# A fused windowed-attention and gated-MLP kernel: its hand-written order of steps is written anew

## Chip, cores and metric

The kernel runs on one core of a Trainium2 chip. The metric is the device time of one execution in microseconds (us). Five engines with queues of their own work side by side, each in the order in which its instructions were issued: PE (matrix products and transposes through the array), DVE, ACT and POOL (vector work; POOL also issues the loads that change the data type), and SP (which only issues transfers).

## The reference

The first half is attention over four batches of 8 heads, 768 positions and 64 channels. A position sees the 128 positions up to itself and the first four ("sinks"). The second half is a gated MLP with a product over the positions, on the attention's output.

```python
scores = scale * np.matmul(q, k.transpose(0, 1, 3, 2))
keep = is_sink | in_window                      # 4 sinks, a window of 128
a = softmax(np.where(keep, scores, -1e9))
x = (a @ v)  as [B, S, H * D]                   # [4, 768, 512]
h = gelu_tanh(x @ w_in)                         # [4, 768, 1024]
u, v = h[..., :512], h[..., 512:]
v_n = (v - mean) / sqrt(var + 1e-6) * g_ln
v_s = einsum('ts,bsd->btd', w_sg, v_n) + b_sg   # w_sg is 768 x 768
out = x + (u * v_s) @ w_out
```

Inputs and output are float32; the kernel works in bf16 and sums in float32.

## The kernel before, in words

**One list is the program.** The string `STEPS` names some 670 steps, and a loop at the end of the kernel issues them one by one. A name is the function, then its indices, then perhaps a letter for the engine (`A` ACT, `D` DVE, `P` POOL). The list is the only thing that sets the order on each engine's queue; waits between engines follow from which tiles the steps read and write. The batches are interleaved by hand: the MLP of one batch runs beside the attention of the next.

**Attention of batch b**, with head pair p (0 to 3):
- `LPQ`/`LPK` (batch 0, SP, float32, one head pair each, cast by `CPQ`/`CPK`), `LQ`/`LK` (other batches, POOL, cast on the way, one position tile each): loads of q and k. `LVH.b.i` loads v for four heads (POOL). `LC` (SP) and `VSM` (DVE) make the sinks' rows of v; `ZERO` sets the columns of ones in the two `v_sb` tiles and clears `ks_sink`; `VSO`, `VSK`, `FILL`, `MASK`, `MASK0`, `IDEN`, `IDEN2` set constants.
- `TQ`/`TK` transpose on PE into a `mm` tile, `EQ`/`EK` copy out to `qT`/`kT`. For batch 0 their second index is the head pair; for 1 and 2 it is a pair of position tiles; for batch 3 `DQ`/`DK` (SP) do it as transposing transfers.
- `QK.b.p.g` writes scores of position-tile group g (0 to 2) into a `sc` tile, `EX` takes the exponential (ACT) into a `P` tile, `MK` masks it (DVE, or two selects on POOL). A fifth index 1 in `QK` adds the mask as a product instead. `KS`, `SK`, `SX` do the same for the sinks.
- `AV.b.p.k` multiplies P with v, whose column of ones gives the sums; `NR` divides and writes `x_sb` (DVE). k runs over three groups of two position tiles in batch 0, over two groups of three in the others.

**MLP of batch b:** `XT`/`XE` (batch 0, PE and a copy) or `XD.b.half` (SP, a transposing transfer) turn x. `MV.b.g` and `MU.b.g` are the products with the two halves of w_in for two position tiles, `GV`/`GU` their gelu (ACT); `BN`, `RS` (a power, POOL), `NM` and `Z` normalise v. `WT`/`WE` transpose w_sg. `SP.b.hf.dc` is the product over positions, `GT` scales it and adds b_sg (DVE), `GM` multiplies by u (DVE or POOL). `OU.b.t` multiplies with w_out, `RA` adds x into an `ot` tile (DVE), `ST` stores it. `SH` stores halves of its columns; for the last tile (batch 3, tile 5) `OH` and `RH` also work by halves. `LW.0` loads the half of w_in that `MV` reads, `LW.1` the other, `LWS` w_sg, `LWO` w_out, `LG` g_ln, `LB` b_sg, `GTR`/`GCP` turn g_ln.

**Tiles.** PSUM has two `sc` tiles (two banks each) and four `mm` tiles (one bank each); a step that needs one takes the next in turn (`fresh`), and must wait until whoever read it last is done. `P` has 10 tiles, `ot` 6, `gtmp` 4, `vt` 3; q, k, v, their transposes, x and z have two each, one per batch in turn.

**Constant products.** `HM.n` makes the next `fresh` issue n products with the zero tile `warm` into the fresh tile first. They compute nothing that is kept.

**Table loads.** ACT holds one table of functions at a time; exponential and gelu are in different ones. `TBL.G` and `TBL.E` run a one-column activation ahead of need.

```python
    def fresh(ring, key):
        t = ring.new(key)
        for _ in range(pre[0]):
            nc.tensor.matmul(t if ring is mm_ring else t[:, 0, :], warm[:, 0:128], warm, start=True, stop=True)
        pre[0] = 0
        return t
```

Of the kernel before, what the change touches and what calls it, by code (L numbers as in the profile page):

```python
# [45 lines left out]
RA.0.3 DK.3.0 SP.1.0.0 RA.0.4 SX.2.0 EX.2.0.1 SP.1.0.1 GT.1.0.0 DQ.3.0 EX.2.1.1 GM.1.0.0.D SP.1.1.0 MK.2.0.1.P
GT.1.0.1 QK.2.2.1 ST.0.3 GT.1.1.0 QK.2.3.1 GM.1.0.1.P DQ.3.1 EX.2.2.1 AV.2.0.0 SP.1.1.1 MK.2.1.1.D EX.2.3.1 MK.2.2.1.P
NR.2.0.0 AV.2.1.0 QK.2.0.2 DQ.3.2 QK.2.1.2 KS.3 EX.2.0.2 MK.2.3.1.P NR.2.1.0 SP.1.1.2 GT.1.1.1 EX.2.1.2 OU.0.5
MK.2.0.2.P GT.1.1.2 ST.0.0 ST.0.4 QK.2.2.2 RA.0.5 QK.2.3.2 MK.2.1.2.P EX.2.2.2 AV.2.2.0 AV.2.3.0 NR.2.2.0 SP.1.1.3
# [666 lines left out]
```

## Time and profile before

| | |
|---|---|
| median of 3 runs | 155.8 us (155.4 to 155.85) |
| the profiled execution | 155.89 us, of which its span is 154.2 us |
| busy in the span | PE 145.7 us (95%), DVE 122.9 (80%), ACT 100.0 (65%), POOL 99.7 (65%) |
| PE products | 1540, weight loads 1554 |
| granted clock | 1.0 |
| loads by POOL (q0) | 11.01 MB in 64608 packets |
| transfers by SP (q1) | 13.41 MB in 22552 packets |

The span runs from the first to the last instruction. A line such as `L483` is a line of the kernel: the scores are L483 (L478 adds a mask), their exponential L488, masks L495 on DVE and L498/L501 on POOL, AV is L524/L528/L531, NR L540/L541, MV L566, MU L607, SP L627, GT L632, GM L637, OU L644, RA L648, OH L657, RH L661; loads by POOL are L225 (q, k), L271 (v), L277 (w_in), L282 (w_sg), L285 (w_out); the constant products are L190, TBL is L309, and copies and casts L199 (ACT), L200 (DVE) and L204 (POOL). In the lines of the page's second part each digit is the busy share of a fortieth of the span, in tenths.

### The profile page before, as it was taken

The numbers are of one execution on the slowest core, as the hardware profiler recorded it, in microseconds if no ns is written. First come the engines' busy times: TensorE is split into PE (matmuls) and PEld (weight loads), VectorE is DVE, ScalarE is ACT, GpSimd is POOL, SyncE is SP. The second block draws the span as 40 slices with busy tenths as digits, with TensorE's granted clock in tenths as the row PEclk, the third lists the DMA queues.
The fourth block names the chain that finished last, engine by engine and source line by source line (L and its number), as shares of the span: only waits on it lengthen the run. The fifth ranks groups of instructions, "written<-read, shape, count | busy, mean of one in ns | idle before, by whom it ended". The sixth has DMA issues, their size and how long they took to land.

```text
span 154.2 us, 3867 instructions
## 1 busy us (share of the span) xinstructions
PE 145.7 (95%) x1540; PEld 94.5 (61%) x1554; DVE 122.9 (80%) x296; ACT 100.0 (65%) x117; POOL 99.7 (65%) x127
## 2 busy tenths in 40 slices
PE   6899899999999988999899999999999999999990
...
GB/s 158 305 351 157 154 195 204 166 189 211 148 141 154 185 155 140 147 150 156 156 223 250 81 276 177 185 190 81 211 72 1 105 221 73 150 54 20 0 203 206
DMA packets 87178, 24.67 MB, mean 160 GB/s; under 512 B 78772, under 2 KB 84920, under 8 KB 87160
## 3 DMA queue, kind: packets, MB, share of 16 engines
q0 software_dynamic: 64608, 11.01, 95.7%
q1 hardware_dynamic: 22552, 13.41, 33.0%
q8 instruction: 12, 0.20, 0.5%
q14 instruction: 6, 0.05, 0.1%
...
## 4 chain that ended last, share of the span: by engine, by line
PE 54%; POOL 18%; DMA 15%; ACT 4%; DVE 4%; issue 2%; SPq 1%; DVEq 0%; ACTq 0%; POOLq 0%
PE mm L627 15%; DMA v_sb<-in_v_dram 11%; PE mm L644 10%; PE sc L566 9%; PE sc L607 8%; POOL q L225 5%; POOL k L225 4%; DMA uT<-in_k_dram 4%; PE sc L483 4%; PE mm L524 3%; POOL v_sb L271 3%; PE mm L528 2%; POOL wsg_gated L637 2%; POOL P L498 2%; POOL P L501 2%
## 5 line engine op out<-in xcount | busy, mean ns | idle before, releaser
L488 ACT ACTIVATE P<-sc 128x1024 bf16<-128x1024 f32 (+1 forms) x48 | 43.4, 952 | 10.3 <-PE sc L483 10.1
L627 PE MATMUL mm<-wsgT,z 128*128 128x384 bf16 x192 | 34.4, 327 | 0.3 <-ACT z L597 0.3
L627 PEld LDWEIGHTS <-z 128*128 128x128 bf16 x192 | 17.6, 98 | 12.5 <-issue 0.7
L570 ACT ACTIVATE vt<-sc 128x1024 f32<-128x1024 f32 x12 | 12.3, 1027 | 18.4 <-PE sc L566 18.4
L632 DVE SCALAR_TENSOR_TENSOR gtmp<-mm,g_sb,b_bc 128x384 bf16<-128x384 f32 x32 | 19.0, 610 | 4.2 <-PE mm L627 4.0
L637 POOL TENSOR_TENSOR wsg_gated<-gtmp,uT 128x384 bf16<-128x384 bf16 x15 | 14.9, 1006 | 11.3 <-DVE gtmp L632 11.2
L607 PE MATMUL sc<-xT,w_in_sb 128*128 128x256 bf16 x192 | 22.1, 273 | 0.0
L566 PE MATMUL sc<-w_in_sb,xT 128*128 128x512 bf16 x92 | 21.8, 379 | 0.2
L644 PE MATMUL mm<-w_out_sb,wsg_gated 128*128 128x512 bf16 x85 | 21.2, 379 | 0.5
L498 POOL TENSOR_SCALAR_AFFINE_SELECT P<-P 128x512 bf16<-128x512 bf16 x21 | 13.7, 653 | 11.4 <-ACT P L488 11.4
L607 PEld LDWEIGHTS <-w_in_sb 128*128 128x128 bf16 x192 | 18.7, 98 | 2.9
L579 DVE BATCH_NORM_STATS2 st<-vt 128x6 f32<-128x512 f32 x24 | 15.4, 685 | 6.1 <-ACT vt L570 6.0
L541 DVE TENSOR_TENSOR x_sb<-mm,rcp 128x384 bf16<-128x384 f32 (+1 forms) x36 | 18.5, 513 | 1.2
L588 POOL TENSOR_TENSOR rs<-rs,neg_half 128x4 f32<-128x4 f32 (+1 forms) x8 | 7.1, 882 | 15.8 <-DVE rs L583 14.4
L225 POOL DMA_DIRECT2D k<-in_k_dram x18 | 16.4, 924 | 1.3 <-DMA v_sb<-in_v_dram 1.3
L648 DVE TENSOR_TENSOR ot<-mm,x_sb 128x512 f32<-128x512 f32 x23 | 15.4, 683 | 2.2 <-PE mm L644 2.2
L225 POOL DMA_DIRECT2D q<-in_q_dram x18 | 16.8, 956 | 0.0
L524 PE MATMUL mm<-v_sb,P 128*128 128x65 bf16 x192 | 16.1, 194 | 0.6 <-DVE x_sb L541 0.4
L524 PEld LDWEIGHTS <-P 128*128 128x128 bf16 x192 | 14.5, 97 | 2.5 <-DMA v_sb<-in_v_dram 0.6
L528 PE MATMUL mm<-v_sb,P 128*128 128x65 bf16 x160 | 15.4, 193 | 0.4 <-POOL P L501 0.4
L612 ACT ACTIVATE uT<-sc 128x1024 bf16<-128x1024 f32 x12 | 12.2, 1024 | 5.1 <-PE sc L607 5.1
L566 PEld LDWEIGHTS <-xT 128*128 128x128 bf16 x96 | 9.2, 98 | 10.1
...
## 6 DMA issues: line engine op xcount, KB each, us to landing
...
```

The costliest lines, as they stand in the source:

```text
L225: return nc.gpsimd.dma_start(out=dst.rearrange("p (h d) -> p h d", h=H), in_=heads(src, b, i))
L488: nc.scalar.activation(out=P.new((b, p, g))[:, :, 0:w], in_=sc_ring[b, p, g][:, :, 0:w], func=AF.Exp, scale=scale)
L498: nc.gpsimd.affine_select(out=p4[:, :, :, 0:128], in_=p4[:, :, :, 0:128], compare_op=ALU.is_ge, fill=0.0, base=0, pattern=[[0, 2], [0, 2], ...
L524: nc.tensor.matmul(av[:, il, hl, :], pt[:, hl, c:c + 128], vb[:, h, i, :], start=first, stop=False)
L528: nc.tensor.matmul(av[:, il, hl, :], pt[:, hl, c:c + 128], vb[:, h, i - 1, :], start=False, stop=(i < 2 and il == n - 1 and hl == 1))
L541: nc.vector.tensor_mul(x_sb.get(b)[:, i0:i0 + n, 128 * p:128 * (p + 1)].rearrange("p t (h d) -> p t h d", h=2), av[:, :, :, 0:Dh], rcp[:, ...
L566: nc.tensor.matmul(hp[:, jl, :], xT[b][:, 2 * g + jl, c, :], w_in_sb[:, c, d_half:2 * d_half], start=(c == 0), stop=(c == KD - 1))
L607: nc.tensor.matmul(hp[:, dc // 2, 256 * (dc % 2):256 * (dc % 2 + 1)], w_in_sb[:, c, 128 * dc:128 * (dc + 1)], xT[b][:, 2 * g:2 * g + 2, c, :],
L627: nc.tensor.matmul(ps[:, 0:NH], z[b][:, si, 128 * dc:128 * (dc + 1)], wsgT[:, si, NH * hf:NH * (hf + 1)], start=(si == 0), stop=(si == NT ...
L632: nc.vector.scalar_tensor_tensor(out=gtmp.new((b, hf, dc)), in0=mm_ring["g", b, hf, dc][:, 0:NH], scalar=g_sb[:, dc:dc + 1], in1=b_bc[:, N ...
L637: (nc.vector if e == "D" else nc.gpsimd).tensor_mul(gated(b, hf)[:, dc, :], gtmp[b, hf, dc], uT[b][:, dc, NH * hf:NH * (hf + 1)])
L644: nc.tensor.matmul(ps, gated(b, hf)[:, dc, 128 * tl:128 * (tl + 1)], w_out_sb[:, dc, :], start=(dc == 0), stop=(dc == KU - 1))
```

## The change

The list is written in a new order. Nearly every step keeps its name: the same loads, products, activations and stores are issued, on other places of their queues. In detail:
- `HM` asks for 15 constant products instead of 21 (8, 2, 1, 2, 2 instead of 9, 4, 1, 3, 1, 3).
- `ZERO` stands second, ahead of all loads.
- Of the casts of batch 0, q of pair 1 goes to POOL, k of pair 0 to DVE; k of pair 2 moves from ACT to POOL, k of pair 3 from POOL to DVE. On SP, `LG` moves up and the loads alternate between q and k.
- On POOL, `LW.0` and `LW.1` follow `LVH.0.1` directly; `LQ.1.0` comes behind them and `LQ.1.1` behind three masks.
- `LVH.2.1` is issued with the loads of batch 2's k, and six loads of batch 3's q and k before `LVH.2.0`; `LK.3.5` comes behind `RS.2.2`.
- Masks: 24 on DVE and 20 on POOL (23 and 21); GM: 16 and 16 (17 and 15); Z: 14 on DVE and 10 on ACT (15 and 9); copies of q and k after their transposes: 11 on DVE and 9 on ACT (10 and 10).
- In batches 1 and 2 `SP` begins with a product of the hf = 1 half; `MU.1.0` comes ahead of `MV.1.0`.
- `TBL` takes a number, so that each such step has a name of its own; the steps stand in other places, two of them (`TBL.G.3`, `TBL.E.3`) one after the other ahead of `GV.3.0`.
- At the end `RH.3.5.0` stands ahead of `OH.3.5.1`, and six of the last eight GM are on POOL. `OH` takes the tile that is held, if there is one, so either half may come first.

The diff, cut to the stretches that matter here:

```diff
 STEPS = """
-WARM LPQ.0 FILL LPK.0 LPK.1 LPQ.1 LPQ.2 LG MASK LPK.2 LPK.3 CPQ.0.A VSK LPQ.3 IDEN CPK.0.A IDEN2 MASK0 HM.9 TQ.0.0
-TK.0.0 EQ.0.0.D EK.0.0.A VSO HM.4 QK.0.0.0 ZERO CPK.1.P QK.0.0.1.1 EX.0.0.0 LVH.0.0 EX.0.0.1 QK.0.0.2.1 CPQ.1.D TK.0.1
-EX.0.0.2 LC CPQ.2.D LVH.0.1 TQ.0.1 MK.0.0.0.D EK.0.1.A HM.1 TQ.0.2 EQ.0.1.D EQ.0.2.A HM.3 QK.0.1.0 CPK.2.A CPK.3.P
-QK.0.1.1.1 EX.0.1.0 LQ.1.0 CPQ.3.D TK.0.2 EX.0.1.1 TK.0.3 EK.0.2.D LQ.1.1 TQ.0.3 EK.0.3.A GTR EQ.0.3.D LW.0 HM.1
-QK.0.2.0 QK.0.2.1 EX.0.2.0 LK.1.0 KS.0 VSM.0 HM.3 SK.0.2 EX.0.2.1 SK.0.1 MK.0.2.0.D AV.0.0.0 LW.1 QK.0.3.0.1
-MK.0.1.0.D SX.0.1 SX.0.2 QK.0.3.1 MK.0.2.1.P GCP.D NR.0.0.0 EX.0.3.0 AV.0.0.1 AV.0.1.0 AV.0.1.1 NR.0.0.1 EX.0.3.1
-QK.0.1.2 NR.0.1.0 AV.0.2.0 AV.0.3.0 EX.0.1.2 MK.0.3.1.P NR.0.1.1 QK.0.2.2 AV.0.2.1 NR.0.2.0 EX.0.2.2 TQ.1.0 NR.0.3.0
-MK.0.1.2.P QK.0.3.2 AV.0.3.1 EQ.1.0.A NR.0.2.1 XT.0.0 NR.0.3.1 LWS.0 AV.0.0.2 EX.0.3.2 TBL.G AV.0.1.2 XE.0.0.D LK.1.1
-XT.0.1 MK.0.2.2.D MV.0.0 XE.0.1.A LK.1.2 NR.0.0.2 MK.0.3.2.D LK.1.3 NR.0.1.2 AV.0.2.2 AV.0.3.2 LQ.1.2 NR.0.2.2 GV.0.0
-MV.0.1 NR.0.3.2 LQ.1.3 BN.0.0 LWS.1 XT.0.2 GV.0.1 MU.0.1 XE.0.2.A BN.0.1 WT.0 GU.0.1 TK.1.0 MV.0.2 RS.0.1 EK.1.0.A
-LK.1.4 NM.0.1 WE.0.A WT.1 GV.0.2 LK.1.5 TK.1.1 MU.0.2 LB.P EK.1.1.A BN.0.2 Z.0.0.A LK.2.0 WT.2 GU.0.2 MU.0.0 WE.1.D
-RS.0.2 WE.2.D Z.0.1.A LQ.2.0 NM.0.2 Z.0.2.A Z.0.3.D Z.0.4.D WT.3 LQ.2.1 WT.4 GU.0.0 TBL.E WE.3.D WT.5 LQ.1.4 Z.0.5.D
+WARM ZERO LPQ.0 CPQ.0.A FILL LPK.0 IDEN LG LPQ.1 LPK.1 IDEN2 LPQ.2 HM.8 TQ.0.0 MASK LPK.2 CPK.0.D EQ.0.0.A LPQ.3 MASK0
+CPQ.1.P TK.0.0 EK.0.0.A HM.2 QK.0.0.1.1 HM.1 QK.0.0.2.1 EX.0.0.1 TQ.0.1 QK.0.0.0 CPQ.2.D CPK.1.P EX.0.0.2 LVH.0.0
+EX.0.0.0 VSK EQ.0.1.D CPK.2.P MK.0.0.0.D LPK.3 TK.0.1 EK.0.1.A LVH.0.1 TQ.0.2 CPQ.3.D EQ.0.2.A CPK.3.D QK.0.1.1.1
+QK.0.1.0 LW.0 HM.2 TK.0.2 TQ.0.3 EX.0.1.1 TK.0.3 LW.1 EX.0.1.0 EK.0.2.A QK.0.2.1 VSO GTR LC EQ.0.3.A EX.0.2.1 LQ.1.0
+EK.0.3.D GCP.D KS.0 QK.0.2.0 HM.2 SK.0.1 QK.0.3.0.1 EX.0.2.0 SX.0.1 MK.0.1.0.D LWS.0 VSM.0 EX.0.3.0 LK.1.0 QK.0.3.1
+EX.0.3.1 MK.0.2.1.P AV.0.0.0 AV.0.0.1 AV.0.1.0 MK.0.2.0.D SK.0.2 QK.0.1.2 NR.0.0.0 NR.0.0.1 NR.0.1.0 AV.0.1.1 EX.0.1.2
+SX.0.2 AV.0.3.0 QK.0.3.2 NR.0.1.1 AV.0.2.0 MK.0.3.1.P QK.0.2.2 MK.0.1.2.P AV.0.3.1 EX.0.3.2 LK.1.1 NR.0.3.0 NR.0.2.0
+AV.0.2.1 NR.0.3.1 LK.1.2 XT.0.0 NR.0.2.1 MK.0.3.2.D AV.0.0.2 AV.0.1.2 XT.0.1 XE.0.0.A EX.0.2.2 XE.0.1.D AV.0.3.2
+MV.0.0 NR.0.0.2 MK.0.2.2.D AV.0.2.2 GV.0.0 LQ.1.1 LQ.1.5 NR.0.1.2 NR.0.3.2 LK.1.3 NR.0.2.2 BN.0.0 LQ.1.4 LWS.1 MV.0.1
+GV.0.1 BN.0.1 TBL.G.1 XT.0.2 MU.0.1 XE.0.2.A GU.0.1 RS.0.1 WT.1 MV.0.2 LQ.1.2 TK.1.0 WE.1.A GV.0.2 WT.0 NM.0.1 Z.0.3.A
+Z.0.0.A MU.0.0 LQ.1.3 TQ.1.0 VSM.2 LB.P EK.1.0.D BN.0.2 LK.1.4 LK.2.1 RS.0.2 VSM.1 Z.0.1.A MU.0.2 TQ.1.2 GU.0.0 WT.2
+GU.0.2 Z.0.2.D WE.0.D EQ.1.0.D NM.0.2 EQ.1.2.D TK.1.1 WE.2.D Z.0.5.D LK.1.5 QK.1.0.0 QK.1.1.0 WT.3 EK.1.1.A Z.0.4.D
+LQ.2.0 WE.3.D WT.4 EX.1.0.0 WT.5 KS.1 LVH.1.0 WE.4.D SP.0.0.0 TQ.1.1 LK.2.0 SP.0.0.2 QK.1.2.0 WE.5.D EX.1.1.0
...
-SP.0.1.2 GT.0.1.1 EX.1.1.2 LK.2.4 GM.0.1.0.D AV.1.0.0 MK.1.3.1.D AV.1.1.0 LK.2.5 GM.0.0.3.D QK.1.2.2 GT.0.1.2 QK.1.3.2
-EX.1.2.2 SP.0.1.3 NR.1.0.0 MK.1.1.2.P EX.1.3.2 NR.1.1.0 AV.1.2.0 AV.1.3.0 MK.1.0.2.P GT.0.1.3 QK.2.0.0 QK.2.1.0
-NR.1.2.0 EX.2.0.0 OU.0.0 MK.1.2.2.P NR.1.3.0 TK.2.1 RA.0.0 AV.1.0.1 XD.1.0 EK.2.1.A MK.1.3.2.P AV.1.1.1 NR.1.0.1
-AV.1.2.1 EX.2.1.0 GM.0.1.2.P NR.1.1.1 AV.1.3.1 NR.1.2.1 QK.2.2.0 LK.3.0 QK.2.3.0 EX.2.2.0 OU.0.1 NR.1.3.1 GM.0.1.3.P
-EX.2.3.0 TBL.G OU.0.2 XD.1.1 RA.0.1 GM.0.1.1.P TK.2.2 MK.2.3.0.D TQ.2.1 LVH.2.0 TQ.2.2 EQ.2.1.D MV.1.0 EQ.2.2.D LQ.3.0
-EK.2.2.D LQ.3.1 VSM.2 MU.1.0 GV.1.0 MK.2.1.0.D LVH.2.1 BN.1.0 MV.1.1 GU.1.0 LQ.3.2 RA.0.2 LQ.3.3 MK.2.0.0.D MV.1.2
-GV.1.1 MK.2.2.0.D LK.3.1 KS.2 LK.3.2 BN.1.1 MU.1.1 GV.1.2 LK.3.3 BN.1.2 RS.1.1 MU.1.2 GU.1.1 LQ.3.4 NM.1.1 Z.1.0.A
+AV.1.0.0 GM.0.0.3.D NR.1.1.0 QK.1.1.2 QK.1.3.2 MK.1.0.2.D AV.1.3.0 EQ.2.0.A EX.1.3.2 GT.0.1.2 NR.1.0.0 GM.0.0.1.P
+NR.1.3.0 MK.1.3.2.D LQ.2.3 AV.1.0.1 AV.1.2.0 SP.0.1.3 EX.1.1.2 QK.2.1.0 NR.1.0.1 QK.2.0.0 NR.1.2.0 MK.1.2.2.P
+GM.0.1.2.P XD.1.0 OU.0.0 AV.1.2.1 MK.1.1.2.D GT.0.1.3 LK.3.3 AV.1.1.1 EX.2.1.0 RA.0.0 LK.2.4 NR.1.2.1 LK.2.5 LQ.2.4
+EX.2.0.0 QK.2.3.0 NR.1.1.1 LQ.3.2 QK.2.2.0 LQ.2.5 KS.2 AV.1.3.1 NR.1.3.1 LQ.3.1 LQ.3.0 OU.0.2 EX.2.2.0 GM.0.1.0.P
+OU.0.1 LQ.3.3 RA.0.2 LQ.3.5 EX.2.3.0 TQ.2.1 TK.2.1 LVH.2.0 RA.0.1 MU.1.0 GU.1.0 EK.2.1.D MV.1.0 TBL.G.2 GV.1.0 XD.1.1
+MK.2.0.0.D MK.2.3.0.D MV.1.1 GM.0.1.1.D MV.1.2 BN.1.0 EQ.2.1.A GV.1.1 BN.1.1 RS.1.1 GM.0.1.3.P MU.1.1 TK.2.2 GV.1.2
+MU.1.2 OU.0.3 BN.1.2 NM.1.1 Z.1.0.D EK.2.2.D Z.1.1.D TQ.2.2 GU.1.1 Z.1.3.A RS.1.2 NM.1.2 RA.0.3 GU.1.2 MK.2.2.0.D
...
-EX.2.3.2 NR.2.3.0 QK.3.0.0 MK.2.3.2.P QK.3.1.0 GT.1.1.3 XD.2.0 EX.3.0.0 AV.2.0.1 MK.2.2.2.D AV.2.1.1 EX.3.1.0 NR.2.0.1
-AV.2.2.1 GM.1.1.3.P ST.0.1 NR.2.1.1 AV.2.3.1 ST.0.2 ST.0.5 GM.1.1.0.P SK.3.0 NR.2.2.1 QK.3.2.0 QK.3.3.0 NR.2.3.1
-EX.3.2.0 GM.1.1.2.P SP.1.0.2 EX.3.3.0 XD.2.1 SP.1.0.3 GT.1.0.2 SX.3.0 TBL.G MK.3.3.0.D MV.2.0 GM.1.0.2.P DK.3.1
-GM.1.1.1.D LK.3.4 MK.3.0.0.D OU.1.3 LVH.3.0 GV.2.0 OU.1.4 RA.1.3 LVH.3.1 OU.1.5 ST.1.3 RA.1.4 GT.1.0.3 MV.2.1 ST.1.4
-MK.3.1.0.D LK.3.5 BN.2.0 GM.1.0.3.P MV.2.2 GV.2.1 BN.2.1 MU.2.1 GV.2.2 BN.2.2 RS.2.1 MU.2.0 GU.2.1 NM.2.1 RA.1.5
+GM.1.0.0.D KS.3 EX.3.0.0 NR.2.2.1 EX.3.2.0 GT.1.0.2 GM.1.1.3.P QK.3.1.0 EX.3.1.0 XD.2.0 QK.3.3.0 ST.0.3 GM.1.0.2.D
+GT.1.0.3 SK.3.0 MK.3.1.0.D LVH.3.0 XD.2.1 ST.0.4 SX.3.0 OU.1.3 OU.1.4 EX.3.3.0 MV.2.0 GM.1.0.3.D GV.2.0 RA.1.3 LK.3.2
+LVH.3.1 LK.3.4 MV.2.1 BN.2.0 MV.2.2 GV.2.1 GV.2.2 MU.2.0 BN.2.1 BN.2.2 DK.3.1 GM.1.0.1.P OU.1.5 RS.2.1 NM.2.1 VSM.3
+GU.2.0 RA.1.4 Z.2.3.D MU.2.2 MU.2.1 OU.1.1 Z.2.1.A RS.2.2 ST.0.5 GU.2.2 Z.2.0.D GU.2.1 OU.1.0 MK.3.2.0.D Z.2.2.D
+NM.2.2 Z.2.4.D RA.1.5 QK.3.0.1 QK.3.1.1 Z.2.5.A SP.2.1.0 RA.1.1 LK.3.5 OU.1.2 SP.2.0.1 MK.3.3.0.D EX.3.0.1 MK.3.0.0.D
...
-NR.3.2.0 NR.3.3.0 EX.3.3.2 TBL.G SP.2.0.3 MK.3.2.2.P GT.2.0.2 XD.3.0 AV.3.0.1 GT.2.0.3 MK.3.3.2.P AV.3.1.1 NR.3.0.1
-AV.3.2.1 GM.2.0.3.P NR.3.1.1 AV.3.3.1 SP.2.1.3 GM.2.0.2.D GM.2.1.1.P NR.3.2.1 OU.2.0 NR.3.3.1 GT.2.1.3 XD.3.1 OU.2.1
-RA.2.0 GM.2.1.3.P OU.2.2 GM.2.1.2.D SH.2.0.0 SH.2.0.1 RA.2.1 MV.3.0 RA.2.2 SH.2.1.0 SH.2.1.1 OU.2.3 GV.3.0 OU.2.4
-BN.3.0 MV.3.1 RA.2.3 RA.2.4 MV.3.2 SH.2.3.0 SH.2.3.1 GV.3.1 SH.2.2.0 SH.2.2.1 SH.2.4.0 SH.2.4.1 BN.3.1 OU.2.5 GV.3.2
-MU.3.2 BN.3.2 RS.3.1 MU.3.1 GU.3.2 NM.3.1 RS.3.2 NM.3.2 Z.3.0.D Z.3.1.A MU.3.0 Z.3.2.D Z.3.3.A Z.3.4.A Z.3.5.D RA.2.5
-SH.2.5.0 SH.2.5.1 SP.3.1.0 GU.3.0 SP.3.1.1 GU.3.1 GT.3.1.0 SP.3.1.2 GM.3.1.0.D GT.3.1.1 SP.3.1.3 GM.3.1.1.D GT.3.1.2
-SP.3.0.0 GM.3.1.2.D SP.3.0.1 GT.3.0.0 GT.3.1.3 SP.3.0.2 GT.3.0.1 GM.3.1.3.P SP.3.0.3 GM.3.0.0.D GM.3.0.1.P GT.3.0.2
-OU.3.3 GM.3.0.2.D GT.3.0.3 OU.3.4 GM.3.0.3.D RA.3.3 OU.3.0 RA.3.4 ST.3.3 OU.3.1 RA.3.0 ST.3.4 OU.3.2 ST.3.0 RA.3.1
-OH.3.5.0 OH.3.5.1 ST.3.1 RA.3.2 ST.3.2 RH.3.5.0 SH.3.5.0 RH.3.5.1 SH.3.5.1
+MK.3.2.2.P SP.2.0.3 NR.3.1.1 EX.3.3.2 MK.3.3.2.P AV.3.2.1 TBL.G.3 ST.1.0 ST.1.1 AV.3.3.1 XD.3.0 GT.2.0.3 NR.3.2.1
+GM.2.1.2.D NR.3.3.1 TBL.E.3 GM.2.0.2.P GM.2.0.3.P SP.2.1.3 OU.2.2 OU.2.0 GT.2.1.3 OU.2.1 GM.2.1.3.D XD.3.1 MV.3.0
+OU.2.4 RA.2.1 RA.2.0 GV.3.0 MV.3.1 MV.3.2 GV.3.1 MU.3.1 GV.3.2 BN.3.0 BN.3.1 RS.3.1 MU.3.2 RA.2.2 BN.3.2 GU.3.1 OU.2.3
+SH.2.2.0 NM.3.1 Z.3.2.A MU.3.0 Z.3.0.D RS.3.2 OU.2.5 NM.3.2 RA.2.3 Z.3.3.A RA.2.4 Z.3.5.D Z.3.1.A Z.3.4.D GU.3.2
+SP.3.1.1 SH.2.3.0 GT.3.1.1 RA.2.5 SH.2.0.0 GU.3.0 SP.3.1.2 SH.2.5.0 GT.3.1.2 SH.2.1.1 SH.2.5.1 SP.3.0.3 SP.3.1.3
+GT.3.0.3 GM.3.1.1.P SP.3.1.0 TBL.G.4 GT.3.1.3 GM.3.1.3.D GM.3.1.2.P GM.3.0.3.P SP.3.0.1 GT.3.1.0 SH.2.2.1 SH.2.3.1
+SP.3.0.0 GT.3.0.0 SH.2.0.1 SH.2.4.0 SH.2.1.0 GT.3.0.1 SP.3.0.2 GM.3.1.0.P OU.3.3 GM.3.0.0.P GT.3.0.2 RA.3.3 GM.3.0.2.D
+GM.3.0.1.P ST.3.3 OU.3.4 OU.3.0 RA.3.4 RA.3.0 OU.3.1 RA.3.1 OU.3.2 OH.3.5.0 SH.2.4.1 ST.3.4 RA.3.2 ST.3.0 ST.3.1
+RH.3.5.0 ST.3.2 OH.3.5.1 SH.3.5.0 RH.3.5.1 SH.3.5.1
 """
...
-    def TBL(func):
+    def TBL(func, turn):
         nc.scalar.activation(out=touch, in_=neg_half[:, 0:1], func=AF.Exp if func == "E" else AF.Gelu_apprx_tanh)
...
     def OH(b, t, h):
         hf, tl = t // 3, t % 3
-        ps = mm_ring["o", b, t] if h else fresh(mm_ring, ("o", b, t))
+        ps = mm_ring["o", b, t] if ("o", b, t) in mm_ring.held else fresh(mm_ring, ("o", b, t))
         for dc in range(KU):
```

More of the change, by code (lines that the diff above doesn't have):

```diff
@@ L46 @@
[L46 to L49, printed above, removed]
-EX.2.3.2 NR.2.3.0 QK.3.0.0 MK.2.3.2.P QK.3.1.0 GT.1.1.3 XD.2.0 EX.3.0.0 AV.2.0.1 MK.2.2.2.D AV.2.1.1 EX.3.1.0 NR.2.0.1
```

25 lines of the change are left out of this document (14 added, 11 removed).

## The prediction

> **What bounds the kernel now.** First the page, then the table of stretches: where is PE not full?
>
> ```profile
> span 154.2 us, 3867 instructions
> ...
> PE   6899899999999988999899999999999999999990
> ```
>
> ```profile
> 0.00:5.00 5.00, 3.75 (x13) 1.30 (x15) 2.65 (x14) 2.12 (x2) 1.76 (x10) 1.00 0.57 182
> ...
> 15.00:20.00 5.00, 4.33 (x84) 2.88 (x83) 4.49 (x15) 4.87 (x8) 4.09 (x7) 1.00 2.81 160
> ...
> 50.00:60.00 10.00, 8.99 (x155) 6.62 (x155) 8.75 (x23) 6.37 (x8) 8.68 (x13) 1.00 1.99 156
> ...
> 110.00:120.00 10.00, 10.00 (x147) 7.13 (x144) 8.69 (x21) 7.11 (x8) 9.13 (x15) 1.00 0.14 43
> ...
> 150.00:154.20 4.20, 0.51 (x5) 0.20 (x3) 1.12 (x3) 0.00 (x0) 0.00 (x0) 1.00 0.60 214
> ```
>
> The number behind the comma is PE's busy time. From about 23 us (the first product with w_in) to 150 us PE is full but for some holes, the largest in 50 to 60. So three places can move the time: how early PE becomes full, the holes, and the tail. PE's own work stays the same but for six constant products. The chain of waits from 5 to 20 us tells what sets the start, and PE's timeline where that ends:
>
> ```profile
> 1.81 5.80 DMA uT<-in_k_dram
> 7.61 0.09 issue
> 7.69 0.79 POOL k L204
> 8.48 8.04 DMA v_sb<-in_v_dram
> ```
>
> ```profile
> 19.44 0.14 PEld L524 LDWEIGHTS <-P 128*128 128x128 bf16 x3 [0.56 <-DMA v_sb<-in_v_dram]
> ```
>
> POOL casts k of head pair 1 when it lands (7.69), then issues the first half of v, which lands at 16.52; PE waits for the second half until 19.44. From there PE runs its queue with hardly a gap to MV.0.0, whose products start at 23.6. The holes, in POOL's and PE's timelines:
>
> ```profile
> 44.38 0.82 POOL L285 DMA_DIRECT2D w_out_sb<-in_moe_w_out_dram  x1
> 45.12 1.84 POOL L225 DMA_DIRECT2D k<-in_k_dram  x2
> 46.88 2.72 POOL L225 DMA_DIRECT2D q<-in_q_dram  x3
> ...
> 51.85 1.82 POOL L225 DMA_DIRECT2D k<-in_k_dram  x2 [1.32 <-DMA v_sb<-in_v_dram]
> ```
>
> ```profile
> 55.83 0.40 PE L382 MATMUL mm<-iden,k 128*128 128x128 bf16 x4 [0.37 <-DMA k<-in_k_dram]
> ```
>
> POOL stands 1.32 us until an older v load has landed (it is the eighth issue behind that load), four masks of 1.2 us each follow on POOL, and PE waits for k, for w_out (0.4 in the list of waits) and for the last mask. The tail, in the timeline of 148 to 154:
>
> ```profile
> 149.47 1.04 PE L657 MATMUL mm<-w_out_sb,wsg_gated 128*128 128x256 bf16 x8
> 149.67 0.69 DVE L648 TENSOR_TENSOR ot<-mm,x_sb 128x512 f32<-128x512 f32 x1 [0.17 <-PE mm L644]
> 150.55 0.76 DVE L661 TENSOR_TENSOR ot<-mm,x_sb 128x256 f32<-128x256 f32 x2 [0.18 <-PE mm L657]
> ```
>
> DVE is free at 150.36, yet RH.3.5.0, the add of the first half, starts at 150.55, when all eight products of L657, both halves, are over (150.51). It waits for the second half too, which lies in other columns of the same PSUM tile.
>
> **The change, part by part.** The sum is made against the profiled execution: 155.89 us, 154.2 of span and 1.7 around it; the median of the three runs is 155.8. "PE work" below is the sum of PE's steps at their own pace in this trace (MU 1.75, MV 1.71, SP 1.03, OU 0.87, AV 0.26 to 0.58, a pair of QK 0.55).
>
> *Free edits.* Of the six products with `warm`, five cost some 0.25 us (four took 1.04) and one of the cold first group 0.41 (nine took 3.71), all before 16 us, where PE waits for casts and copies: 0. The ones columns take DVE 0.5 us, now ahead of FILL; POOL's masks follow with 4 us in hand: 0. w_in: no wait names it, and PE first wants it at 23.6, so its loads gain nothing where they go. On POOL's queue they pass LQ.1.0, but TQ.1.0, which reads that, moves behind 13 us of PE work: 0. LK.3.5 goes behind RS.2.2 (103 us): 5.9 to land and 3.1 for DK.3.2, as the same steps took, make 112; QK.3.0.2 wants it at 113: 0, with 1 us in hand. Copies change engines: summed up to MV.1.0, ACT has 4.6 us less, DVE 1.4 more, both below PE. The table loads (1.28 us each) that TBL asked for now mostly come with the first activation that needs one, and the TBL behind it only touches, 0.2. TBL.G.3 and TBL.E.3 add two loads ahead of GV.3.0, where ACT stood idle 6.3 us: 0.
>
> *The first v, +0.7.* POOL must now cast q and k of pair 1 before it, and that k is the fourth large load on SP, no longer the third. LG's issue (0.41) ahead of it costs nothing: SP had issued five loads by 3.3 us, and the third landed at 7.7. The fourth one's cast started at 8.68: 8.68 + 0.83 = 9.5 instead of 8.48, +1.0. VSK (0.4) and a cast (0.83) now part the two issues of v, but the second half queues behind the first anyway (16.52 to 19.4). A later start meets less of SP's loads, which end at 12.8: between +0.4 and +1.4 for the second half; I take +0.7, as the first half should come nearer to the second's 2.9 us.
>
> *From v to MV.0.2, +0.6.* AV.0.3.2 (0.45) comes ahead of MV.0.0 and TQ.1.0 (0.47) goes behind: even. But AV.0.3.2 needs a mask that stands on DVE behind NR.0.2.1, the last one ready (+0.3), and between MU.0.1 and MV.0.2 PE has only WT.1 (0.4), while ACT must do GV.0.1 1.02, the touch 0.2 and XE.0.2 1.0 (+0.3). 0 if these overlap; 1.0 if EX.0.3.2, whose scores now stand on PE behind the wait for v, holds XE.0.0 up too.
>
> *The holes at 50 to 63, -1.3.* PE's start times less its work grow there from 10.7 (AV.1.2.0) to 12.2 (MV.1.0), so 1.5 are lost. Now w_out lands before OU.0.0 wants it, TK.2.1 stands 4.8 us of PE work later, and MK.1.3.2 and MK.1.1.2 go to DVE. Bounds -1.6 and 0 (if loads stop POOL's masks again); a PE that comes 1.3 late finds these waits shorter anyhow, so I lean to the lower end.
>
> *Transposes by DMA, +0.6.* LQ.3.0 to LQ.3.3, LQ.3.5, LK.3.3 and LVH.2.1 move ahead: POOL has 5.8 us more to do before MV.1.0. XD.1.1, which MV.1.1 needs, now runs beside these loads. Such transposes landed in 3.7 to 5.2 us, this one, beside a single load, being the slowest. Between AV.1.3.1 and MV.1.1 PE has 6.2 us of work (7.4 before), and the way over NR.1.3.1 (1.0) and XD.1.1 (5.2) takes 6.2: no slack. One more such difference (1.5) is the upper bound, 0 the lower.
>
> *Middle, 0.* SP.1.1.0 waits less for its last Z than SP.1.0.0 did (-0.4). SK.3.0 takes the PSUM tile that NR.2.2.1 frees, now behind NR.2.3.1, GM.1.0.0 and KS.3 on DVE (+0.9); before, PE lost 0.5 there over masks. Bounds -0.9 and +0.9.
>
> *Tail, +0.95.* Six of the last eight GM go to POOL (1.0 each; 0.4 on DVE), and GM.3.0.2 stands on DVE behind RA.3.3 (0.68): OU.3.0 waits +0.3 (0 to 0.6). RH.3.5.0 now precedes OH.3.5.1. By the row above, halves of one tile are ordered as wholes, so OH.3.5.1 must wait for it: RA.3.2 ends at 150.37, then 0.42, 0.7 for the four products (two thirds of 1.04) and 0.42 more, with hand-overs 151.95 instead of 151.31: +0.65; 0 if only columns counted. SH.2.4.1 goes behind ST.3.3, and RA.3.2 needs its `ot` tile: landing 1.8 later just meets it, 0 (up to 0.5).
>
> The Trainium skill (PSUM — Partial Sum Buffer, section PSUM bank collisions raise a hardware error) says to guard PSUM by bank and quadrant, not by address. That speaks against this edit, and the wait at 150.55 agrees; by address the sum would be 0.65 less.
>
> Sum: 0.7 + 0.6 - 1.3 + 0.6 + 0 + 0.95 = +1.55: 157.4.
>
> **Rivals.** (a) *The holes swallow it: faster.* They are set by loads and POOL, not by PE, and the new order thins them too. With XD.1.1 in time, -0.4 at SP.1.1.0, -0.5 for the masks of batch 2 and a tail of +0.3: 1.3 - 1.6 - 0.9 + 0.3 = -0.9, 155.0. It decides if PE has caught up at MV.1.1. For it: ACT's lighter load; against: the tail. 0.20. (b) *Even:* the same with the full tail, about 155.7: 0.12. (c) *The transposes collide.* XD.1.0 and XD.1.1 are 1.5 late each, and RS.1.1 stands behind LVH.2.0: +0.6 becomes +2.5, 159.3. For it: a fuller queue; against: POOL issues some loads only after masks, which leaves gaps. 0.17. (d) *A colder start.* In the trace nine products ran at 0.41 us each and TQ.0.0 behind them at full rate. Eight end at 4.55 instead of 4.96; if PE then stayed at half rate for another 3.7 us (the nine's own time), TQ.0.0, TK.0.0 and two QK, 2.7 in all, would take double, somewhat over half of it behind copies: +1.1 on the sum, 158.5. 0.05.
>
> The Trainium skill (TensorE: Matmul & The Clock Gate, Part 1) lets the gate open after a busy window of about 3.4 us whose phase is free. By that rule the eight, 3.3 us at 0.41 each, may just miss a window, which is (d); the profile's clock row shows 9 throughout and can't tell.
>
> **The numbers.** The forecast has 0.46: 157.4, its own range 156.3 to 158.8 by the bounds above. To leave out no more than 2 in 10 the range reaches past (a) and (c): 154.8 to 159.9. A difference within 0.3% (0.5 us), about what a measurement of this kernel can tell, counts as the same: faster 0.20, same 0.12, slower 0.68.
>
> **What would show it.** PE's wait for the second half of v ends near 20.1 and MV.0.0 starts past 24 (else the first two terms fall); in 50 to 63 no wait for w_out or k; SK.3.0 right after NR.2.2.1; at the end L657 in two groups with RH.3.5.0 between. I am wrong if MV.1.1 starts before 65.8, or if PE waits over 2 us ahead of it.

## The result, and the profile after

The kernel with the new order takes 166.32 us (median of 4 runs, 165.84 to 166.65), the kernel before beside it 155.82: a ratio of 1.066, 95% interval 1.061 to 1.072. The prediction was 157.4 with a range up to 159.9, so the sign was right and the size, 1.6 us instead of 10.5, was not. A median here is of all runs of a kernel, while a ratio compares only the runs within 1.5% of the fastest of their kernel. The profiled execution took 166.59 us, with a span of 164.9, 10.7 more than before.

The page first. PE's row has two deep notches that were not there, and the clock row dips behind each.

```profile
span 164.9 us, 3854 instructions
...
PE   6898899999999998399999993799999999999991
...
PEclk9999999999999999879999999569999999999999
```

The table of stretches gives them their places (PE's busy time behind the comma; the third number from the end is the granted clock):

```profile
50.00:60.00 10.00, 10.00 (x159) 6.99 (x156) 9.72 (x25) 7.78 (x10) 9.98 (x13) 1.00 1.81 168
60.00:70.00 10.00, 6.68 (x49) 4.01 (x48) 4.58 (x10) 3.88 (x5) 8.53 (x10) 0.94 1.99 153
70.00:80.00 10.00, 10.00 (x80) 6.42 (x79) 7.35 (x19) 6.76 (x7) 5.32 (x6) 0.89 1.72 123
...
100.00:110.00 10.00, 6.29 (x19) 2.41 (x18) 3.18 (x9) 2.17 (x3) 1.03 (x1) 0.66 1.27 164
```

The holes at 50 to 60 are gone (PE 10.00 busy, 8.99 before). In their place PE misses 3.3 us in 60 to 70 and 3.7 in 100 to 110. The chain of waits names the cause; its columns are start, length, what:

```profile
60.01 8.62 DMA xT<-x_sb
68.67 4.45 PE sc L566 x12
...
95.62 8.47 DMA xT<-x_sb
104.14 5.30 PE sc L566 x12
```

These are XD.1.1 and XD.2.1, the transposing transfers of the second halves of x. PE's timeline shows what happens at MV.1.1 and at MV.2.1:

```profile
62.60 2.75 PE L566 MATMUL sc<-w_in_sb,xT 128*128 128x512 bf16 x12
68.67 4.45 PE L566 MATMUL sc<-w_in_sb,xT 128*128 128x512 bf16 x12 [3.31 <-DMA xT<-x_sb]
```

```profile
97.68 2.75 PE L566 MATMUL sc<-w_in_sb,xT 128*128 128x512 bf16 x12
104.14 5.30 PE L566 MATMUL sc<-w_in_sb,xT 128*128 128x512 bf16 x12 [3.71 <-DMA xT<-x_sb]
```

Twelve products take 2.75 us ahead of each wait and 4.45 and 5.30 behind it: half the pace, as the granted clock says (0.50 in a finer table of stretches from 69 to 72 and from 103 to 109 us). So each late transfer costs twice: the wait, and then some us at half rate. What stands beside the transfers is in POOL's timeline; of the changed kernel:

```profile
57.40 2.70 POOL L225 DMA_DIRECT2D k<-in_k_dram  x3
60.06 4.40 POOL L225 DMA_DIRECT2D q<-in_q_dram  x5
...
93.29 1.48 POOL L271 DMA_DIRECT2D v_sb<-in_v_dram  x1
94.76 0.89 POOL L225 DMA_DIRECT2D k<-in_k_dram  x1
95.62 1.44 POOL L271 DMA_DIRECT2D v_sb<-in_v_dram  x1
```

and of the kernel before, whose XD.2.1 was issued at 91.09, beside its SP's row:

```profile
93.16 0.94 POOL L225 DMA_DIRECT2D k<-in_k_dram  x1
94.09 2.83 POOL L271 DMA_DIRECT2D v_sb<-in_v_dram  x2
```

```profile
91.09 1.43 SPq L557 DMA_TRANSPOSE xT<-x_sb  x1
```

Before, a load of k (LK.3.4) was issued 2.1 us behind the transfer and LVH.3.0 3.0 us behind it; now LVH.3.0 goes 2.3 us and a load of k 0.9 us ahead of it, and LVH.3.1 in the same moment.

Where the time goes, by PE's start times less the PE work done by then, the measure that the prediction used for the holes (each step's change is the difference of two neighbours):

| at | before | after | difference | change |
|---|---|---|---|---|
| MV.0.0 | 10.65 | 10.93 | +0.28 | +0.28 |
| MV.1.1 | 12.21 | 11.45 | -0.76 | -1.04 |
| MU.1.2 | 12.24 | 16.79 | +4.55 | +5.31 |
| MV.2.0 | 13.49 | 17.32 | +3.83 | -0.72 |
| MU.2.2 | 13.59 | 23.99 | +10.40 | +6.57 |
| OH.3.5.0 | 12.61 | 23.03 | +10.42 | +0.02 |
| end of the span | | | +10.70 | +0.28 |

The two transfers make 11.9 us. All else together is a gain of 1.2.

### The profile page after: what moved, and what is told of

Same layout as the page of the kernel before. It is cut to its first block, busy times and chain, and to the rows that moved or that the text cites. A ratio compares the mean times of both kernels' runs of the same rounds, so it can differ in the third digit from the quotient of the medians.

```text
span 164.9 us, 3854 instructions
## 1 busy us (share of the span) xinstructions
PE 150.2 (91%) x1548; PEld 94.7 (57%) x1548; DVE 123.0 (75%) x297; ACT 100.8 (61%) x117; POOL 99.8 (61%) x127
## 4 chain that ended last, share of the span: by engine, by line
PE 55%; DMA 20%; DVE 13%; SPq 4%; issue 3%; POOL 3%; DVEq 0%
PE sc L566 12%; PE mm L627 12%; PE sc L607 12%; DMA xT<-x_sb 10%; PE mm L644 6%; DVE x_sb L541 5%; DMA v_sb<-in_v_dram 4%; PE sc L483 4%; DMA uT<-in_k_dram 3%; SPq L664 3%; DVE gtmp L632 3%; DMA out_dram<-ot 2%; PE mm L382 2%; PE mm L524 2%; DVE P L495 2%
## 5 line engine op out<-in xcount | busy, mean ns | idle before, releaser
L566 PE MATMUL sc<-w_in_sb,xT 128*128 128x512 bf16 x96 | 26.4, 432 | 7.0 <-DMA xT<-x_sb 7.0
L627 PEld LDWEIGHTS <-z 128*128 128x128 bf16 x192 | 17.7, 98 | 11.9 <-issue 0.4
L607 PE MATMUL sc<-xT,w_in_sb 128*128 128x256 bf16 x192 | 22.8, 274 | 0.0
L644 PE MATMUL mm<-w_out_sb,wsg_gated 128*128 128x512 bf16 x92 | 22.2, 379 | 0.0
L566 PEld LDWEIGHTS <-xT 128*128 128x128 bf16 x96 | 10.0, 108 | 20.8 <-DMA xT<-x_sb 8.0
L637 POOL TENSOR_TENSOR wsg_gated<-gtmp,uT 128x384 bf16<-128x384 bf16 x16 | 15.4, 972 | 9.2 <-DVE gtmp L632 9.1
L498 POOL TENSOR_SCALAR_AFFINE_SELECT P<-P 128x512 bf16<-128x512 bf16 x20 | 13.1, 653 | 10.3 <-ACT P L488 10.3
L524 PE MATMUL mm<-v_sb,P 128*128 128x65 bf16 x192 | 16.4, 194 | 0.8 <-DMA v_sb<-in_v_dram 0.8
L225 POOL DMA_DIRECT2D q<-in_q_dram x18 | 16.2, 914 | 0.0
L528 PE MATMUL mm<-v_sb,P 128*128 128x65 bf16 x160 | 15.6, 194 | 0.0
```

The source lines that it names most:

```text
L225: return nc.gpsimd.dma_start(out=dst.rearrange("p (h d) -> p h d", h=H), in_=heads(src, b, i))
L524: nc.tensor.matmul(av[:, il, hl, :], pt[:, hl, c:c + 128], vb[:, h, i, :], start=first, stop=False)
L528: nc.tensor.matmul(av[:, il, hl, :], pt[:, hl, c:c + 128], vb[:, h, i - 1, :], start=False, stop=(i < 2 and il == n - 1 and hl == 1))
L566: nc.tensor.matmul(hp[:, jl, :], xT[b][:, 2 * g + jl, c, :], w_in_sb[:, c, d_half:2 * d_half], start=(c == 0), stop=(c == KD - 1))
L607: nc.tensor.matmul(hp[:, dc // 2, 256 * (dc % 2):256 * (dc % 2 + 1)], w_in_sb[:, c, 128 * dc:128 * (dc + 1)], xT[b][:, 2 * g:2 * g + 2, c, :],
L627: nc.tensor.matmul(ps[:, 0:NH], z[b][:, si, 128 * dc:128 * (dc + 1)], wsgT[:, si, NH * hf:NH * (hf + 1)], start=(si == 0), stop=(si == NT ...
```

## The experiments

Theory T: loads by POOL beside a transposing transfer make it late, PE's wait lowers the clock, and nothing else of the new order costs much. Rival R: the transfers are late for a reason of their own. Rival C: the slow products come from the DMA traffic, not from the wait. The diffs show only the steps that move, with "..." for what is left out; in 3 and 6 they show only the places that the steps move to.

**1. The loads moved behind steps that need the transfer's result.** First XD.1.1 alone, then XD.2.1 alone, then both:

```diff
 XD.1.0
-LK.3.3 LQ.3.2 LQ.3.1 LQ.3.0 LQ.3.3 LQ.3.5 LVH.2.0
 XD.1.1
...
 RS.1.1 GM.0.1.3.P
+LVH.2.0 LQ.3.2 LQ.3.3
...
 RS.1.2
+LQ.3.0 LQ.3.1 LQ.3.5 LK.3.3
```

> Theory T: XD.1.1 took 8.6 us from issue to landing because POOL's loads were in flight beside it; PE then stood 3.7 us at MV.1.1 and its next 12 products ran at half rate (4.45 us instead of 2.6), which is the clock's answer to the idle time. With seven loads of batch 2 and 3 (LVH.2.0 and six of q and k) moved behind RS.1.1 and RS.1.2, which wait for products of this very xT, XD.1.1 lands within 6 us, PE waits at most 1 us and stays at full rate: about 4.5 us less than the changed kernel, 161.8. XD.2.1 stays as late as it is. Rival R (the transpose is late for a reason of its own, its long issue on SP or the store behind it): still over 8 us to landing, 166 us.

172.85 us, ratio 1.102 (1.091 to 1.112): a miss. XD.1.1 took 7.1 us, with the last four loads of batch 2 still beside it; PE waited 1.8 us and kept its clock. But the moved loads pushed RS.1.2 back (PE waited 2.2 us for z, 1.7 and 0.5, and the clock fell), they came in beside the transposes of q and k (DQ.3.1 landed at 88.9), and XD.2.1 took 9.8 us. The run speaks for T only in XD.1.1's own time.

```diff
 LQ.3.4
+LK.3.2
...
-LVH.3.0
 XD.2.1
...
-LK.3.2 LVH.3.1 LK.3.4
...
 RS.2.1
+LVH.3.0
...
 RS.2.2
+LVH.3.1 LK.3.4
```

> Theory T for XD.2.1 (8.5 us to landing, PE idle some 4 us, 12 products 5.3 us instead of 2.6): with LVH.3.0, LVH.3.1 and LK.3.4 behind RS.2.1 and RS.2.2, and LK.3.2 earlier behind LQ.3.4, it lands within 4 us, MV.2.1 doesn't wait, and the time falls by about 6.4 us to 159.9. XD.1.1 stays as it is. Rival R: still over 8 us to landing, 166 us.

163.14 us, 1.044 (1.036 to 1.052). XD.2.1 took 3.65 us instead of 8.47, and PE ran through MV.2.0 to MV.2.2 in one piece, 24 products in 5.34 us:

```profile
97.25 5.34 PE L566 MATMUL sc<-w_in_sb,xT 128*128 128x512 bf16 x24
```

That is 3.2 us less than the changed kernel, half of the 6.4 expected. By MU.2.2 the whole 6.6 us had come back; 1.7 were lost again because LK.3.4 now came late for QK.3.0.2, and 1.2 at OU.3.1, where RA.3.3 waited for a store of batch 2 to let go of its `ot` tile. R falls.

> The loads of both experiments moved. Theory T: the two gains add up, 166.3 - 4.5 - 6.4 = 155.4, about the time of the kernel before; PE's work at MV.2.0 then stands some 0.5 us ahead of it, which the tail takes back. Rival R: 166. If one of the moved loads becomes late itself, 157 to 158.

166.28 us, 1.065 (1.057 to 1.072). XD.2.1 3.7 us, XD.1.1 7.4; the losses of the first run of this group stayed. Moving loads late is no remedy: whoever reads them is late in turn.

**2. The waits filled with constant products.** `HM.12` ahead of MV.1.1, `HM.16` ahead of MV.2.1, nothing else.

> The changed kernel with 12 constant products ahead of MV.1.1 and 16 ahead of MV.2.1. Theory T: both transposes land as late as before, but PE stands only some 1.2 us instead of 3.7 and 4.1, so the clock isn't lowered: the products behind the waits go back to 0.22 us each, and 1.9 + 2.9 us come back: 161.5, granted clock 1.0 throughout. Rival C (the products are slow because the DMA traffic or the transposes' writes hold them, not because PE stood idle): still 0.37 to 0.44 us each and no gain, 166 us.

163.23 us, 1.050 (1.042 to 1.057), 3.1 less than the changed kernel (4.8 expected); the profiled run took 162.49, 4.1 less. The transfers were as late as before (7.5 and 9.1 us), the clock stayed at 1.0, and the products behind the second wait ran at full pace:

```profile
97.38 3.62 PE L190 MATMUL sc<-warm 128*128 128x512 bf16 x16
100.83 1.03 PE L566 MATMUL sc<-w_in_sb,xT 128*128 128x512 bf16 x4
102.76 2.76 PE L566 MATMUL sc<-w_in_sb,xT 128*128 128x512 bf16 x12 [0.90 <-DMA xT<-x_sb]
```

Twelve in 2.76 us instead of 5.30, with the same transfers and loads around them: C falls.

**3. The loads moved early, the transfer left in a gap.** Batch 2's loads go ahead of POOL's masks, three GM follow LQ.2.5, and LVH.2.0, LVH.2.1 and batch 3's loads come behind them; for XD.2.1 the k loads go early and v behind RS.2.1.

```diff
 LWO
+LK.2.3 LK.2.2 LQ.2.3 LK.2.4
...
 GM.0.1.2.P
+LQ.2.5
...
+GM.0.1.3.P GM.0.1.1.P LVH.2.0 LQ.3.2 LQ.3.3 LVH.2.1 LQ.3.0 LQ.3.1
...
 LQ.3.4
+LK.3.2 LK.3.4 LK.3.5
...
 RS.2.1
+LVH.3.0
...
 RS.2.2
+LVH.3.1
```

> Another arrangement for XD.1.1 alone: the loads of batch 2's last tiles go ahead of POOL's masks, as early as the queue lets them, and LVH.2.1, LVH.2.0 and batch 3's loads follow three GM on POOL, which cover the time in which XD.1.1 is issued. Theory T: the transposes then run between two bunches of loads; XD.1.1 lands within 5 us instead of 8.6 (the first arrangement left four loads beside it, and it took 7.1), PE waits less than 1 us at MV.1.1 and keeps its clock: 166.3 - 3.4 - 1.9 = 161.0. Rival R: over 7 us to landing whatever is beside it, 164 to 166.

169.57 us in the median, 3.3 more than the changed kernel (164.7 to 171.2; the profile is of the fastest run). XD.1.1 landed in 3.65 us, PE ran MV.1.0 to MV.1.2 without a wait, as T says, and so came to XD.2.1 when both halves of v of batch 3 were being loaded: that transfer took 11.2 us and PE waited 6.4. The gain of the first place was paid back at the second.

> As in the experiment on XD.2.1, but LK.3.4 and LK.3.5 are loaded early too, behind LQ.3.4, so that DK.3.2 isn't late (there PE waited 1.7 us for it). Theory T: XD.2.1 lands in 3.7 us, the 6.4 us at MV.2.1 come back and none is lost at QK.3.0.2: 159.9, or 160.9 if the last stores of batch 2 hold the ot tiles as they did there (OU.3.1, 1.1 us).

159.63 us, 1.024 (1.016 to 1.031), as forecast. XD.1.1 still took 8.8 us there, and PE waited 2.6 for it.

> The two arrangements together. Theory T: they add up, 166.3 - 5.3 - 6.4 = 154.6, or 155.7 with the stores' 1.1 us at OU.3.1: the rest of the new order costs nothing against the kernel before. If something else of the new order costs time that the two waits covered, 157 or more.

159.99 us, 1.025 (1.017 to 1.034), 5.4 more than forecast. No wait for either transfer; but eight loads in a row made the masks of batch 2 late, and one of them met POOL on DVE. DVE's timeline, then POOL's:

```profile
88.13 3.44 DVE L495 TENSOR_TENSOR P<-P,mask 128x1024 bf16<-128x1024 bf16 x1
```

```profile
88.38 2.63 POOL L637 TENSOR_TENSOR wsg_gated<-gtmp,uT 128x384 bf16<-128x384 bf16 x3
```

The mask (0.68 us otherwise) ended at 91.57, 0.55 after POOL's last product. PE stood 1.8 us for it and then had half rate for 3.4 us; from 89 to 96 us it lost 3.9 in all, by the measure of the table above. Where the rest of the 5.4 went was not settled.

**4. The other way round: the kernel before, made to collide.** Only loads of batch 3 move ahead of XD.2.1: both halves of v, one half, or two loads of k.

```diff
 GM.1.1.3.P
+LVH.3.0
...
 GM.1.1.0.P
+LVH.3.1
...
 XD.2.1
...
-LVH.3.0
...
-LVH.3.1
```

> The kernel before with one thing of the change: LVH.3.0 and LVH.3.1 go to POOL behind GM.1.1.3 and GM.1.1.0, ahead of the issue of XD.2.1. Theory T: XD.2.1 takes about 8 us to landing instead of 4, PE idles some 3.5 us at MV.2.1 and then runs some 2 us of products at half rate: 155.9 + 5 = 161. Rival R (loads beside it don't matter): 156.

> The kernel before with only LVH.3.0 ahead of XD.2.1. Theory Q: some 7 us to landing, PE waits 1 to 1.5 us at MV.2.1, 157.3, or 159 if that wait lowers the clock. Rival A: as long as with both halves, 10 us to landing and 161.

> The kernel before with LK.3.4 and LK.3.5 (128 KB each, some 0.9 us of POOL's queue each) ahead of XD.2.1 in place of the two halves of v (2.9 us of the queue each), which made it 10 us to landing. Theory Q (the transposing transfer gets through only as the loads queued ahead of it are done, so its time grows with them): some 6 us to landing, PE waits under 0.5 us at MV.2.1: 156.2. Rival A (any load beside it disturbs it by the same 4 to 5 us): 8 us or more, a wait of over 2 us and a lowered clock: 159 or more.

| ahead of XD.2.1 | us, ratio (interval) | PE waits at MV.2.1 | next 12 products |
|---|---|---|---|
| LVH.3.0, LVH.3.1 | 161.42, 1.036 (1.030 to 1.042) | 4.00 | 4.45 us |
| LVH.3.0 | 159.22, 1.023 (1.019 to 1.027) | 2.39 | 4.45 us |
| LK.3.4, LK.3.5 | 156.80, 1.006 (1.003 to 1.010) | 0 | full rate |

With one v load PE's row reads

```profile
98.79 4.45 PE L566 MATMUL sc<-w_in_sb,xT 128*128 128x512 bf16 x12 [2.39 <-DMA xT<-x_sb]
```

Moving the two halves gives the kernel before 5.6 of the change's 10.5 us, and moving one of them 3.4. The delay grows with what is queued ahead, though not in proportion: from issue to PE's restart 8.7 us with one half, 10.4 with both, and not over 6.5 with the two k loads. The trace's packets say the same of the transfer itself: its last data packet came 5.9 us after the issue with the two k loads, 7.1 with one half and 7.7 with both, against 3.1 in the kernel before. Of the two readings Q is nearer, and A falls. The run with the two k loads is still 1.0 us (0.4 to 1.5) longer, without a wait at MV.2.1; where that goes was not followed.

**5. Single terms on the kernel before.** The last mask on DVE, as in the change, and the order of the halves at the end:

```diff
-MK.1.3.2.P
+MK.1.3.2.D
```

> The kernel before with the mask MK.1.3.2 on DVE, as the change has it, and nothing else: a test of the term for the holes at 50 to 63 by itself. AV.1.3.1 waited some 0.7 us for this mask, the last of four on POOL, while DVE stood idle at 56.1. Theory T: AV.1.3.1 follows AV.1.2.1 without a wait, NR.1.3.1 and XD.1.1 come 0.7 earlier, and the time falls by 0.4 to 0.8: 155.2. Rival (the next wait takes it over: MV.1.0 or MV.1.1 waits for the transposes as long): 155.9.

161.45 us, 1.038 (1.034 to 1.043): the largest miss, from one letter. DVE's timeline, then POOL's:

```profile
57.43 2.85 DVE L495 TENSOR_TENSOR P<-P,mask 128x1024 bf16<-128x1024 bf16 x1
```

```profile
57.09 0.64 POOL L498 TENSOR_SCALAR_AFFINE_SELECT P<-P 128x512 bf16<-128x512 bf16 x1
57.68 0.63 POOL L501 TENSOR_SCALAR_AFFINE_SELECT P<-P 128x512 bf16<-128x512 bf16 x1
58.29 0.90 POOL L637 TENSOR_TENSOR wsg_gated<-gtmp,uT 128x384 bf16<-128x384 bf16 x1
59.14 0.94 POOL L225 DMA_DIRECT2D k<-in_k_dram  x1
```

The mask took 2.85 us while POOL worked without a pause. NR.1.3.1 and with it XD.1.1 came 3.2 us later than before (1.5 of them this run had lost by AV.1.2.0); POOL, with a mask less, issued LVH.2.0 at 61.9, now ahead of XD.1.1 (63.1). The transfer took 8.3 us, PE waited 2.6, and the clock fell.

```diff
-OH.3.5.1
...
 RH.3.5.0
+OH.3.5.1
```

> The kernel before with OH.3.5.1 behind RH.3.5.0, and nothing else. The prediction's reading (halves of one PSUM tile are ordered as wholes): +0.5 to 0.65 us, 156.4. Rival (only the columns count, or the last store's landing hides it): no difference.

156.33 us, 1.004 (1.001 to 1.007), or 0.6 us (0.1 to 1.1) of 155.9: in the range forecast.

**6. The new order repaired.** As in 3 for both transfers, with fewer loads in a row; then also with the tail of before; then two more runs of the latter, each with its profile.

```diff
+LK.3.3 LQ.3.5
 RS.1.1
...
 LQ.3.4
+LK.3.2
...
 RS.2.1
+LK.3.4 LK.3.5 LVH.3.1
...
 RS.2.2
+LVH.3.0
```

> The changed kernel with POOL's loads arranged so that neither XD.1.1 nor XD.2.1 has them beside it, and without the bunch of eight loads that in the run with both arrangements made the masks of batch 2 late (PE stood there some 2 us, then had half rate for 3.4 us). Theory T: no wait over 1 us is left; what remains of the new order is a gain of about 0.7 at the holes and a loss of about 0.5 in the tail: 155.3 to 156.5. If the new order loses elsewhere than at the transposes, 158 or more.

> The same with the tail as it was before: OH.3.5.1 ahead of RH.3.5.0, and each store of batch 2 right behind its add. Theory T: 0.5 us less than the run beside it from the order of the halves, and up to 1.1 more where the late stores held the ot tiles: 154.5 to 155.8. If the order of the halves is free, no difference.

159.24 us in the median, 155.7 to 165.9; with the tail of before 161.17, 156.6 to 165.2. The kernel before lay between 155.1 and 158.3 beside them. The spread is the kernel's own, so no ratio is given, and what the tail does can't be read from these two. The fastest runs are as forecast; the profile of the second is one of them (156.62): no wait for a transfer, 1.2 us at QK.3.0.2 for the last k.

> The repaired order with the tail of before, a second look: its runs lay between 156.6 and 165.2, and the profiled one was the fastest, without a wait of PE for a transposing transfer. If the spread comes from the same cause, a profile of a longer run shows PE waiting at MV.1.1 or MV.2.1 behind a transfer of over 6 us, with a lowered clock after it. If it comes from the start (constant products that end at another moment of the clock's own rhythm), the clock is at half between 5 and 12 us and the later part is as in the first profile.

> The same kernel, a third look. The same two readings: a wait for a transposing transfer with a lowered clock behind it, or a start at half the clock.

162.07 and 157.21 us. The longer run has the late transfer of the first reading, though without the lowered clock behind it; the shorter one has the slow start of the second. In the longer one DVE met POOL again:

```profile
50.07 1.70 DVE L637 TENSOR_TENSOR wsg_gated<-gtmp,uT 128x384 bf16<-128x384 bf16 x1
...
52.38 1.45 DVE L495 TENSOR_TENSOR P<-P,mask 128x1024 bf16<-128x1024 bf16 x1
...
55.67 1.64 DVE L495 TENSOR_TENSOR P<-P,mask 128x1024 bf16<-128x1024 bf16 x1
```

Three steps of 0.4 to 0.7 us took 4.8 us together. XD.1.1 was issued at 62.63 instead of 60.45 and met LVH.2.0 (61.76): 8.8 us to landing. PE waited 2.2 us for it and went on at full rate (twelve products in 2.76 us). In the shorter one the start was slow; its granted clock was at half until 10.5 us:

```profile
1.25 3.60 PE L190 MATMUL mm<-warm 128*128 128x512 bf16 x8 [1.25 <-DVE warm L306]
4.80 0.85 PE L376 MATMUL mm<-iden,q 128*64 128x128 bf16 x12
6.17 0.85 PE L376 MATMUL mm<-iden,k 128*64 128x128 bf16 x12 [0.52 <-DVE k L200]
```

The transposes behind the eight constant products took 0.85 us instead of 0.53, and MV.0.0 stood 1.5 us further back than in the changed kernel's profile. (The slow transposes alone tell nothing: the fastest run, 156.62, has them too.) Whether these two causes make up the whole spread is open.

No version beat the kernel before.

## Why the prediction was right or wrong

*DMA transposes, +0.6: the step that failed.* The mechanism was named (the transfer runs beside these loads; rival (c)), but its price was bounded by the slowest such transfer in the trace, 5.2 us, plus one more such difference, 1.5. That transfer had one load beside it. In the changed kernel three loads of 128 KB had been issued just before XD.1.1 and one in the same moment, seven more followed while it ran, and it took 8.6 us. The bound extrapolated a queue from a row in which the queue was nearly empty, and from two of that trace's transfers only; the packets of a third, XD.1.0, which ran beside six such loads, end 5.6 us after its issue (3.2 alone) and would have warned.

*XD.2.1 was not in the sum.* The list showed it: LVH.3.0 now stands directly ahead of XD.2.1, where it stood 13 steps behind. The prediction names neither of the two; what a load does to a neighbour on the other queue was asked for XD.1.0 and XD.1.1 only. XD.2.1 took 8.5 us, and its place cost 6.6, more than the place that the sum had.

*The clock.* Rival (d) had the half rate for the start alone. In these runs it came behind every idle time of PE of 2.4 us or more, and behind some from 1.7 on, and it made some 1.7 of the first loss and 2.6 of the second (4.45 and 5.30 against 2.75 for twelve products). A late transfer should have been priced as wait plus half rate, 5 to 6 us, not as the wait. With 5.3 and 6.6 in place of 0.6 the sum is 168.7; the other terms, below, bring it to 166.7 (166.59 in the profiled execution).

*The holes, -1.3:* -1.0 (MV.0.0 to MV.1.1 in the table); no wait for w_out or k was left in 50 to 63, as forecast. But the mask on DVE, to which the prediction gave no price, is free only while POOL leaves gaps.

*The first v, +0.7:* +0.3. Its first half was issued 0.6 later (forecast 1.0) and yet landed earlier, at 16.31; the second half landed at 19.51 instead of 19.39. *From v to MV.0.2, +0.6:* +0.05. Of the signs named, the wait's end near 20.1 and MV.0.0 past 24 both failed (19.56 and 23.65). *Middle, 0:* -0.7, inside its bounds; SK.3.0 did start right behind the last operation of NR.2.2.1 (95.61 behind 95.56). *Rival (d)* was not there in the profiled run of the change, and its premise, that nine constant products are safe and eight are not, does not hold: of the 12 profiles with eight, five have the transposes behind them at 0.85 us (and a sixth a granted clock of 0.50 from 8 to 11 us), but so have four of the six with nine. The half rate at the start varies from run to run with either.

*The tail, +0.95:* +0.3. OU.3.0 did not wait, and the order of the halves gave what it was said to, less what the last store's landing gave back:

```profile
159.90 0.60 PE L657 MATMUL mm<-w_out_sb,wsg_gated 128*128 128x256 bf16 x4
161.17 0.60 PE L657 MATMUL mm<-w_out_sb,wsg_gated 128*128 128x256 bf16 x4 [0.68 <-DVE ot L661]
```

From OH.3.5.0's first product to the end of RH.3.5.1 it took 2.33 us instead of 1.84; the last store's landing gave back 0.2 (2.66 us instead of 2.85). The second half's four products wait for the first half's add.

*The range* held rival (c) only at its underestimated price. "I am wrong if MV.1.1 starts before 65.8, or if PE waits over 2 us ahead of it" came true in both halves: it started at 64.33, and the wait, in its middle, was 3.3 us.
